# Last stage of a fused attention, MLP and SwiGLU kernel: which queue loads its operands, how many buffers they have, and where the last outputs leave from

## The chip, the cores and the metric

The kernel runs on one core of a Trainium2 chip. Its time is device microseconds from one launch; the time before is 1744.82 us, the median of three runs (1743.07 to 1746.58).

## The reference

Three layers in a row, all in float32:

```python
kv  = einsum('bhsd,bhse->bhde', k, v)              # 8 batches, 8 heads, 576 tokens, 64 wide
out = einsum('bhsd,bhde->bhse', q, kv)
x   = out / sqrt(mean(out**2) + 1e-6) * g_norm     # -> 4608 tokens x 512
h   = x @ w_in                                     # 512 x 2048
x   = (h * clip(h + 3, 0, 6) / 6) @ w_out          # 2048 x 512
g   = x @ w_gate                                   # 512 x 1536
out = (silu(g) * (x @ w_val)) @ w_out2             # 1536 x 512
```

The change lies in the last product, `(...) @ w_out2`, and in what is fetched for it.

## The kernel before, in words

Every float32 operand of a product is split in two, `hi` (rounded to the PE's short float32 form, by ScalarE) and `lo` (the rest, by VectorE), and a product is three matmuls. The layers after the first use a Strassen-like scheme with seven products in place of eight, so the last stage needs seven combinations of the activations: four (`G1`) for its first half, three (`G2`) for its second. The stage before it, `gv_step`, writes these combinations to HBM as `g1d` and `g2d`.

The last stage goes over six blocks of 768 tokens (`j` = 5 down to 0). A block has two halves `h`, a half six steps `q` of two 128-rows each; a step is one *task*, 72 in all. A task of the first half is 24 matmuls of 128x384 (`o2_one`: kinds e, c, d, a), one of the second half 18 (`o2_two`: kinds c, d, a). For each task `g_halves` gets a buffer `graw`, loads it, and splits it: ScalarE makes `gh`, VectorE makes `gl` (lines 107 and 108). `prepare_g(n + 3)` puts this three tasks ahead of the product in the program. Steps 4 and 5 of each half are multiplied together, kind by kind, which needs both loaded.

Before the change `graw` has two buffers and SP's queue issues its loads. The same queue issues the stores of the outputs: `put` transposes an output tile on VectorE (`ot`) and issues four stores; a block has eight tiles, two after its first half (kinds u + v) and six at its end, so 32 stores of 48 KB each.

The matmuls are in the order in which the code issues them. The order on ScalarE, VectorE and the queues is made by a scheduler, and each engine and each queue runs its instructions in that order. The weights of the stage come in six groups of seven tiles (`reload_w2`, 256 KB a tile), named 20 to 25 in the rows; the first two tasks (`g_first`) are loaded one combination at a time into other buffers.

Of the kernel before, what the change touches and what calls it, by code (L numbers as in the profile page):

```python
# [8 lines left out]
F32 = mybir.dt.float32  # L9
F32R = mybir.dt.float32r  # L10
U32 = mybir.dt.uint32
U16 = mybir.dt.uint16
AF = mybir.ActivationFunctionType
ALU = mybir.AluOpType
# [5 lines left out]
def kernel(  # L20
# [27 lines left out]
    nc = tc.nc  # L48
    P = 128
# [5 lines left out]
    KD = DM // P  # L55
# [4 lines left out]
    Q = 32  # L60
# [5 lines left out]
    TH = 384  # L66
    T2 = 2 * TH
    NB2 = NT // T2
    NQ = NF2 // 2
# [17 lines left out]
    wraw = mlp2.enter_context(tc.tile_pool(name="wraw", bufs=3))  # L87
# [14 lines left out]
    def f32(ap):  # L102
        return ap.bitcast(F32)

    def split(hi, lo, src):

        nc.scalar.activation(out=hi, in_=src, func=AF.Copy)  # L107
        nc.vector.tensor_tensor(out=lo, in0=src, in1=f32(hi), op=ALU.subtract)  # L108
# [21 lines left out]
    g1d = dram.tile([NQ, NB2, P, 4, TH], F32, name="g1d")  # L130
    g2d = dram.tile([NQ, NB2, P, 3, TH], F32, name="g2d")
# [22 lines left out]
    def w_slot(name, dtype):  # L154
        return wpool.tile([P, KD, P], dtype, tag="w", name=name)
# [508 lines left out]
    big = {}  # L664
    x_ops = {}

    def load_x1(j):
        x = big["xr"].tile([P, KD, T2], F32, tag="xr", bufs=1, name=f"xr_{j}")
        nc.sync.dma_start(out=x, in_=x1d[:, :, j * T2:(j + 1) * T2])
        return x  # L670
# [49 lines left out]
    G1, G2 = ("T2", "T1", "T3", "B11"), ("T4", "B21", "B22")  # L720
# [67 lines left out]
    def flat(o):  # L788
        return o.rearrange("p k f -> p (k f)")

    def w2_operands(q, tiles):
        w2[q] = {
            key: tuple(flat(o) for o in ops) for key, ops in operands(tiles).items()
        }
# [3 lines left out]
    def slot(name, dtype=F32):  # L798
        return flat(w_slot(name, dtype))

    def g_first(j, q):

        for k, key in enumerate(G1):
            n = f"{key}_{j}_{q}"
            raw, hi, lo = slot(f"ra_{n}"), slot(f"gh_{n}", F32R), slot(f"gl_{n}", F32R)
            nc.sync.dma_start(out=raw[:, :TH], in_=g1d[q, j, :, k])
            split(hi[:, :TH], lo[:, :TH], raw[:, :TH])
            g_ops[j, q, key] = hi[:, :TH], lo[:, :TH]

    def g_halves(j, h, q):  # L810

        n = f"{h}_{j}_{q}"
        keys, src = ((G1, g1d), (G2, g2d))[h]
        m = len(keys)
        raw = big["gr"].tile([P, 4, TH], F32, tag="raw", name=f"graw_{n}")[:, :m]
        nc.sync.dma_start(out=raw, in_=src[q, j])
        hi, lo = (
            big["gy" if h else "gx"].tile([P, m, TH], F32R, tag=f"{h}{o}", name=f"g{o}_{n}")
            for o in "hl"
        )  # L820
        split(hi, lo, raw)
        for k, key in enumerate(keys):
            g_ops[j, q, key] = hi[:, k], lo[:, k]

    acc2 = {}

    def o2_product(j, k, qs, b, a, first):

        ops = [(q, g_ops.pop((j, q, b)), w2[q][a]) for q in qs]
        for i in range(2):  # L830
            cs = slice(i * P, (i + 1) * P)
            for q, g, w in ops:
                for n, (a_, b_) in enumerate(((w[0], g[1]), (w[1], g[0]), (w[0], g[0]))):
                    nc.tensor.matmul(
                        acc2[k][i], a_[:, cs], b_,
                        start=first and q == 0 and n == 0, stop=n == 2, skip_group_check=True,
                    )
            yield i, acc2[k][i]
# [19 lines left out]
                    o, ps_ = ("v", ps) if k == "d" else ("u", acc2["e"][i])  # L858
                    nc.vector.tensor_tensor(out=acc2[o][i], in0=acc2[o][i], in1=ps_, op=ALU.add)

    def put(j, o, dm, i, tok):

        t = slot("ot")[:, :TH]
        nc.vector.transpose(out=t, in_=o)
        r0, c0 = j * T2 + tok * TH, dm * 2 * P + i * P
        for n in range(P // Q):
            nc.sync.dma_start(  # L867
                out=out[r0:r0 + TH, c0 + n * Q:c0 + (n + 1) * Q].rearrange(
                    "(i p) c -> p i c", p=Q
                ),  # L870
                in_=t[n * Q:(n + 1) * Q].rearrange("p (i c) -> p i c", c=Q),
            )

    def o2_two(j, qs):

        for k, b, a, dm, tok in (
            ("c", "B22", "S4", 0, 1), ("d", "T4", "A22", 1, 0), ("a", "B21", "A12", 0, 0),
        ):
            for i, ps in o2_product(j, k, qs, b, a, False):
                if qs[-1] == NQ - 1:  # L880
                    o = slot("o")[:, :TH]
                    if k == "a":
                        nc.scalar.activation(out=o, in_=ps, func=AF.Copy)
                    else:
                        nc.vector.tensor_tensor(out=o, in0=acc2["u"][i], in1=ps, op=ALU.add)
                    put(j, o, dm, i, tok)
        if qs[0] == 0:
            for i in range(2):
                o = slot("o")[:, :TH]
                nc.vector.tensor_tensor(out=o, in0=acc2["u"][i], in1=acc2["v"][i], op=ALU.add)  # L890
                put(j, o, 1, i, 1)
# [4 lines left out]
    with tc.manual_schedule(engines={mybir.EngineType.PE}):  # L896
# [13 lines left out]
        for h in range(2):  # L910
            nc.scalar.dma_start(
                out=gn[h * D:(h + 1) * D, :], in_=g_norm.rearrange("(p o) -> p o", o=1)
            )
        for key, f in (("i", 0), ("i", 1), ("i", 2), ("o", 0), ("i", 3), ("o", 1), ("i", 4)):
            src, ld = (w_in, load_w_cols) if key == "i" else (w_out, load_w_rows)
# [220 lines left out]
        def load_second():  # L1136
            if second:
                kind, p, i = second.pop()
                tiles = load_half(kind, p, i, raw2 if i else None)
                if tiles:  # L1140
                    wgv[kind, p] = operands(tiles)
# [33 lines left out]
        for j in range(1, NB):  # L1175
# [3 lines left out]
            for i, p in enumerate(pairs):  # L1179
# [25 lines left out]
                if j == NB - 1:  # L1205
                    if i == NP1 - 2:
                        parts = prepare_x(0, x1, fpool)
# [36 lines left out]
        JO = list(reversed(range(NB2)))  # L1244
# [8 lines left out]
        def reload_w2(q):  # L1253
            tiles = [w_slot(f"2{q}_{i}", F32R) for i in range(7)]
            for i in (2, 3, 4, 5, 0, 1, 6):
                nc.sync.dma_start(out=flat(f32(tiles[i])), in_=w2d[q, i])
            w2_operands(q, tiles)

        for c, (n, j, p) in enumerate(steps):
            i = c % NH  # L1260
            nxt = visits[n + 1][0] if n + 1 < len(visits) else j
            if i == 0 and nxt != j:
                x1 = load_x1(nxt)
            gv_step(c, j, p, x_ops[j])
            while second:
                load_second()
            if i == NH - 1 and nxt != j:
                *_, x_ops[nxt] = prepare_x(nxt, x1)
            if n < NB2:
                m = (n + 1) % NB2  # L1270
                if i < 2:
                    tiles = load_half(*halves[m], i)
                    if i and m:
                        for k, t in enumerate(tiles):
                            nc.sync.dma_start(
                                out=wsd[m - 1, k], in_=f32(t).rearrange("p k f -> p (k f)")
                            )
                    elif i:
                        wgv[halves[0]] = operands(tiles)
                if n == turn:  # L1280
                    for m in (2 * i + 1, 2 * i + 2):
                        if m < 2 * NH:
                            reload(m)
            else:

                m = c - NB2 * NH
                if m < W2_STEPS:
                    tiles = make_w2(m // 2, m % 2)
                    if tiles:
                        for k, t in enumerate(tiles):  # L1290
                            nc.sync.dma_start(out=w2d[m // 2, k], in_=flat(f32(t)))
            m = c - len(steps)
            if m == -3:
                reload_w2(0)
                g_first(JO[0], 0)
            elif m == -2:
                reload_w2(1)
                g_first(JO[0], 1)
            elif m == -1:
                reload_w2(2)  # L1300
                reload_w2(3)

        mlp2.close()
        big["gr"], big["gy"], big["gx"] = (
            ctx.enter_context(
                tc.tile_pool(name=n, bufs=b, side=o, reuse_waits="tile")
            ) for n, b, o in (("gr", 2, "right"), ("gy", 4, "right"), ("gx", 4, "left"))
        )
        tasks = [(j, h, q) for j in JO for h in range(2) for q in range(NQ)]

        def prepare_g(n):
            if 1 < n < len(tasks):
                g_halves(*tasks[n])

        prepare_g(2)
        reload_w2(4)
        reload_w2(5)
        for n, (j, h, q) in enumerate(tasks):
            prepare_g(n + 3)
            if q < NQ - 2:  # L1320
                (o2_two if h else o2_one)(j, (q,))
            elif q == NQ - 1:
                (o2_two if h else o2_one)(j, (q - 1, q))


# [31 lines left out]
```

## Time and profile before

| what | value |
|---|---|
| time, median of three | 1744.82 us |
| the profiled execution | 1744.33 us, its span 1742.5 us |
| TensorE (PE) busy over the span | 1667.6 us, 96% |
| VectorE (DVE), ScalarE (ACT) busy | 1233.9 us (71%), 890.4 us (51%) |
| mean granted TensorE clock | 0.985 |

The span is what the profiler saw from the first to the last instruction; the rest of the time lies around it. A busy PE is not a PE at full pace: matmuls overlap, and one takes longer at a lower granted clock. In the rows L834 is a matmul of the last stage, L816 a load of `graw`, L867 a store of an output, L1256 a load of a weight tile, SPq is SP's queue.

### The profile page before, as it was taken

The page shows a single profiled execution, that of the slowest core. Times are in us where ns is not written, and L with a number is a line of the kernel's source. Part 1 is how long each engine was busy: PE and PEld are TensorE (multiplying, and loading weights), DVE is VectorE, ACT ScalarE, POOL GpSimd, SP SyncE. Part 2 cuts the span into 40 slices and gives each one's busy share as a digit, 9 for nine tenths or more (in the row PEclk, how much of TensorE's full clock was granted, in tenths as well). Part 3 has the DMA queues.
Part 4 walks back from the last instruction along what each step waited for, and adds up shares of the span by engine and source line. Part 5 has one row for each costly group of instructions (what it writes and reads, how often), then busy time and mean ns, then how long its engine had stood idle before and what let it go on. Part 6 is the DMA issues. An engine that isn't in the chain of part 4 may idle for free.

```text
span 1742.5 us, 27207 instructions
## 1 busy us (share of the span) xinstructions
PE 1667.6 (96%) x9884; PEld 1535.1 (88%) x9884; DVE 1233.9 (71%) x2390; ACT 890.4 (51%) x1647; POOL 2.4 (0%) x7
## 2 busy tenths in 40 slices
PE   8999999999999999999999999999999988888887
PEld 4568899999999999998899999999999987888776
DVE  6888987677777776769897776688876544454444
ACT  5875564545444444446675555466655432332322
POOL 0000000000000000000000000000000000000000
PEclk9999999999999999999999999999999989989999
DMA  8885445454445444254576556866545776656665
GB/s 226 275 261 157 128 144 142 155 140 146 130 148 142 141 134 136 90 176 155 191 257 216 195 197 220 283 226 227 198 173 182 268 237 180 180 172 177 169 179 120
DMA packets 302471, 316.92 MB, mean 182 GB/s; under 512 B 160000, under 2 KB 233216, under 8 KB 302336
## 3 DMA queue, kind: packets, MB, share of 16 engines
q1 hardware_dynamic: 297952, 314.13, 57.8%
q8 instruction: 78, 1.28, 0.3%
q10 hardware_dynamic: 4384, 1.05, 0.3%
q14 instruction: 57, 0.47, 0.1%
HBM read 218.10 MB, written 96.99 MB: 181 GB/s over the span
## 4 chain that ended last, share of the span: by engine, by line
PE 72%; DMA 10%; DVE 9%; ACT 4%; SPq 3%; issue 2%; DVEq 0%; ACTq 0%
PE g L607 15%; PE v L607 15%; PE acc L111 7%; PE acc L112 6%; PE acc L113 6%; PE a L607 6%; DMA graw<-g1d 6%; PE c L607 4%; PE d L607 4%; DMA graw<-g2d 3%; DVE gl L108 3%; SPq L867 2%; ACT gh L107 2%; PE h L117 2%; PE kv L290 1%
## 5 line engine op out<-in xcount | busy, mean ns | idle before, releaser
L108 DVE TENSOR_TENSOR gl<-graw,gh 128x1152 fp32r<-128x1152 f32 (+1 forms) x70 | 108.3, 1549 | 173.6 <-ACT gh L107 173.4
L111 PE MATMUL acc<-g,wo 128*128 128x512 f32 x512 | 202.1, 395 | 0.0
L112 PE MATMUL acc<-g,wo 128*128 128x512 f32 x512 | 199.6, 390 | 0.0
L113 PE MATMUL acc<-g,wo 128*128 128x512 f32 x512 | 199.5, 390 | 0.0
L107 ACT ACTIVATE gh<-graw 128x1152 fp32r<-128x1152 f32 (+1 forms) x70 | 92.3, 1322 | 200.9 <-DMA graw<-g1d 137.4
L652 ACT ACTIVATE t<-h,three 128x512 f32<-128x512 f32 x120 | 86.8, 724 | 141.3 <-DVE h L649 107.6
L107 ACT ACTIVATE g<-t 128x512 fp32r<-128x512 f32 x142 | 89.5, 630 | 65.3 <-DVE t L653 55.0
L108 DVE TENSOR_TENSOR g<-t,g 128x512 fp32r<-128x512 f32 x142 | 96.6, 681 | 31.6 <-ACT g L107 30.8
L113 PEld LDWEIGHTS acc<-g,wo 128*128 128x128 f32 x512 | 96.1, 188 | 20.5
L111 PEld LDWEIGHTS acc<-g,wo 128*128 128x128 f32 x512 | 96.2, 188 | 19.9 <-DVE g L108 0.3
L112 PEld LDWEIGHTS acc<-g,wo 128*128 128x128 f32 x512 | 96.2, 188 | 18.3
L653 DVE SCALAR_TENSOR_TENSOR t<-t,h 128x512 f32<-128x512 f32 x120 | 82.3, 686 | 30.7 <-ACT t L652 29.3
L607 PE MATMUL v<-hT,v 128*128 128x384 f32 x288 | 73.6, 336 | 0.0
L750 DVE TENSOR_TENSOR hg<-hg,g 128x384 f32<-128x384 f32 x36 | 19.9, 552 | 59.4 <-PE g L607 28.1
L108 DVE TENSOR_TENSOR lT<-T,hT 128x384 fp32r<-128x384 f32 x88 | 48.5, 554 | 18.1 <-ACT hT L107 17.7
L760 ACT ACTIVATE hg<-hg 128x768 f32<-128x768 f32 x36 | 30.4, 843 | 58.8 <-DVE hg L752 58.8
L767 ACT ACTIVATE hg<-g 128x384 f32<-128x384 f32 x72 | 35.0, 487 | 49.4 <-PE g L607 49.2
L117 PE MATMUL h<-x,w_i 128*128 128x512 f32 x128 | 57.8, 594 | 1.3 <-DVE w_i L201 0.7
L607 PE MATMUL v<-hB,v 128*128 128x384 f32 x216 | 55.1, 336 | 0.0
L607 PE MATMUL a<-T,wh_i 128*128 128x256 f32 x240 | 53.5, 285 | 1.2 <-ACT s L626 1.1
L607 PE MATMUL c<-T,wh_i 128*128 128x256 f32 x240 | 53.0, 283 | 0.0
L607 PE MATMUL d<-T,wh_i 128*128 128x256 f32 x240 | 53.0, 283 | 0.0
(571 smaller groups left out, 5027.5 us busy)
## 6 DMA issues: line engine op xcount, KB each, us to landing
wo<-wod SPq DMA_DIRECT2D x128, 512.0 KB, 3.5
graw<-g1d SPq DMA_DIRECT2D x34, 768.0 KB, 5.1
g1d<-gt SPq DMA_DIRECT2D x108, 192.0 KB, 2.0
graw<-g2d SPq DMA_DIRECT2D x36, 576.0 KB, 4.1
xr<-x1d SPq DMA_DIRECT2D x10, 1536.0 KB, 6.9
g2d<-hv SPq DMA_DIRECT2D x36, 384.0 KB, 2.4
x1d<-x1o SPq DMA_DIRECT2D x36, 256.0 KB, 2.8
out_dram<-ot SPq DMA_DIRECT2D x192, 48.0 KB, 1.8
```

The lines of the kernel that those rows point to most:

```text
L107: nc.scalar.activation(out=hi, in_=src, func=AF.Copy)
L108: nc.vector.tensor_tensor(out=lo, in0=src, in1=f32(hi), op=ALU.subtract)
L111: nc.tensor.matmul(out_, wh, xl, start=start, stop=False)
L112: nc.tensor.matmul(out_, wl, xh, start=False, stop=False)
L113: nc.tensor.matmul(out_, wh, xh, start=False, stop=stop)
L117: nc.tensor.matmul(out_, f32(w), f32(x), start=start, stop=stop)
L607: nc.tensor.matmul(ps, a[:, kk], b[kk] if isinstance(b, list) else b[:, kk], start=first and n == 0, stop=n == 5, skip_group_check=True,)
L652: nc.scalar.activation(out=t, in_=h[i], func=AF.Relu, bias=three[:, 0:1])
L653: nc.vector.scalar_tensor_tensor(out=t, in0=t, scalar=6.0, in1=h[i], op0=ALU.min, op1=ALU.mult)
L760: nc.scalar.activation(out=hg[:, odd], in_=hg[:, odd], func=AF.Silu)
L767: nc.scalar.activation(out=hg[:, o], in_=ps[0], func=AF.Silu)
L867: nc.sync.dma_start(out=out[r0:r0 + TH, c0 + n * Q:c0 + (n + 1) * Q].rearrange("(i p) c -> p i c", p=Q), in_=t[n * Q:(n + 1) * Q].rearrang ...
```

## The change

The load and the split are parted: `g_load` issues the load on ScalarE's queue one task before the split, into three buffers in place of two. Task 2 of the first block is loaded by `g_early` in two halves, on SP's queue, into buffers that the stage before has in use. The weight groups 20 and 21 are asked for earlier and the first two tasks' loads stand one step differently. Steps 4 and 5 are no longer multiplied together in the first half of the first block, and steps 3 to 5 are in the last half of the last block. In the last block the kind `a` is transposed straight from PSUM, without ScalarE's copy, and five of its eight stores go to ScalarE's queue.

```diff
+    def g_load(j, h, q):
+        m, src = ((4, g1d), (3, g2d))[h]
+        raw = big["gr"].tile([P, 4, TH], F32, tag="raw", name=f"graw_{h}_{j}_{q}")[:, :m]
+        nc.scalar.dma_start(out=raw, in_=src[q, j])
+        graw[j, h, q] = raw
+
+    def g_early(j, h, q):
+        graw[j, h, q] = parts = []
+        for i in range(2):
+            raw = wraw.tile([P, KD, P, 2], U32, tag="raw", name=f"graw_{h}_{j}_{q}_{i}")
+            raw = flat(raw.rearrange("p k c t -> p k (c t)").bitcast(F32))
+            raw = raw[:, :2 * TH].rearrange("p (n t) -> p n t", n=2)
+            nc.sync.dma_start(out=raw, in_=g1d[q, j, :, 2 * i:2 * i + 2])
+            parts.append(raw)
+
     def g_halves(j, h, q):
         n = f"{h}_{j}_{q}"
-        keys, src = ((G1, g1d), (G2, g2d))[h]
+        keys, raw = (G1, G2)[h], graw.pop((j, h, q))
         m = len(keys)
-        raw = big["gr"].tile([P, 4, TH], F32, tag="raw", name=f"graw_{n}")[:, :m]
-        nc.sync.dma_start(out=raw, in_=src[q, j])
...
-        split(hi, lo, raw)
+        if isinstance(raw, list):
+            for i, r in enumerate(raw):
+                split(hi[:, 2 * i:2 * i + 2], lo[:, 2 * i:2 * i + 2], r)
+        else:
+            split(hi, lo, raw)
...
+    JO_END = 0
...
-    def put(j, o, dm, i, tok):
+    def put(j, o, dm, i, tok, queues=(0, 0, 0, 0)):
...
-        for n in range(P // Q):
-            nc.sync.dma_start(
+        for n, e in enumerate(queues):
+            (nc.sync, nc.scalar)[e].dma_start(
...
-                    o = slot("o")[:, :TH]
-                    if k == "a":
-                        nc.scalar.activation(out=o, in_=ps, func=AF.Copy)
+                    end = k == "a" and j == JO_END
+                    if end:
+                        o = ps
                     else:
-                        nc.vector.tensor_tensor(out=o, in0=acc2["u"][i], in1=ps, op=ALU.add)
-                    put(j, o, dm, i, tok)
+                        o = slot("o")[:, :TH]
+                        if k == "a":
+                            nc.scalar.activation(out=o, in_=ps, func=AF.Copy)
+                        else:
+                            nc.vector.tensor_tensor(out=o, in0=acc2["u"][i], in1=ps, op=ALU.add)
+                    put(j, o, dm, i, tok, (1, 0, 1, 1 - i) if end else (0, 0, 0, 0))
...
             m = c - len(steps)
-            if m == -3:
+            if m == -6:
                 reload_w2(0)
+            elif m == -4:
+                reload_w2(1)
+            elif m == -3:
                 g_first(JO[0], 0)
             elif m == -2:
-                reload_w2(1)
                 g_first(JO[0], 1)
+                g_early(JO[0], 0, 2)
+                reload_w2(2)
             elif m == -1:
-                reload_w2(2)
                 reload_w2(3)
...
-            ) for n, b, o in (("gr", 2, "right"), ("gy", 4, "right"), ("gx", 4, "left"))
+            ) for n, b, o in (("gr", 3, "right"), ("gy", 4, "left"), ("gx", 4, "right"))
...
         def prepare_g(n):
+            if 2 < n + 1 < len(tasks):
+                g_load(*tasks[n + 1])
             if 1 < n < len(tasks):
                 g_halves(*tasks[n])
...
+            group.append(q)
+            together = 1 if n < NQ else 3 if n >= len(tasks) - NQ else 2
+            if q < NQ - together or q == NQ - 1:
+                (o2_two if h else o2_one)(j, tuple(group))
+                group = []
```

What this does to the order is seen on SP's queue first, where block 5 ends and block 4 begins (`graw_4_1` is block 4, step 1; `ot` are output tiles). Before:

```order
L816 DMA graw_4_0_16311<-g1d 128x1536
L816 DMA graw_4_1_16335<-g1d 128x1536
L816 DMA graw_4_2_16341<-g1d 128x1536
L867 DMA out_dram<-ot 32x12x32 x24
L816 DMA graw_4_3_16431<-g1d 128x1536
L816 DMA graw_4_4_16469<-g1d 128x1536
```

The load of step 3 stood behind the 24 stores of the block's end. Now SP's queue, from the last weight tiles to its end:

```order
L1282 DMA 25_5_16020<-w2d 128x512
L1282 DMA 25_0_16015<-w2d 128x512
L1282 DMA 25_1_16016<-w2d 128x512
L1282 DMA 25_6_16021<-w2d 128x512
L889 DMA out_dram<-ot 32x12x32 x187
```

Nothing but stores is left on it, 187 of 192. The loads are on ScalarE, here where block 4 ends and block 3 begins (L107 is the split's `gh`, L909 the copy of kind a; DMAHW is one of eight semaphores that the transfers of both queues take in turn):

```order
L816 DMA graw_3_1_16725<-g1d 128x1536 [waits DMAHW7_49,DVE_49]
L816 DMA graw_3_2_16749<-g1d 128x1536 [waits DMAHW2_49,DVE_49]
L107 ACTIVATE gh_3_1_16751<-graw_3_1_16725 128x1536 [waits DMAHW7_49]
L816 DMA graw_3_3_16755<-g1d 128x1536 [waits DMAHW4_49,DVE_49]
L107 ACTIVATE gh_3_2_16757<-graw_3_2_16749 128x1536 [waits DMAHW2_49]
L816 DMA graw_3_4_16845<-g1d 128x1536 [waits DMAHW0_49,DVE_49]
L107 ACTIVATE gh_3_3_16847<-graw_3_3_16755 128x1536 [waits DMAHW4_49]
L909 ACTIVATE o<-o2a_4_16443 128x384 [waits PE_49]
L816 DMA graw_3_5_16883<-g1d 128x1536 [waits DMAHW5_49,DVE_49]
L909 ACTIVATE o<-o2a_4_16444 128x384 [waits PE_49]
```

A load now stands between the splits of the two tasks before it, and the two copies of kind a stand behind the split of step 3; before, they stood ahead of it.

At the entry to the stage SP's queue had, behind the last store of the stage before (`gt_35`):

```order
L756 DMA g2d<-gt_35_15940 128x384
L1256 DMA 24_0_15995<-w2d 128x512
L1256 DMA 24_1_15996<-w2d 128x512
L1256 DMA 24_6_16001<-w2d 128x512
L816 DMA graw_5_2_15989<-g1d 128x1536
L1256 DMA 25_2_16011<-w2d 128x512
```

and has now:

```order
L756 DMA g2d<-gt_35_15958 128x384
L1282 DMA 23_6_15968<-w2d 128x512
L1282 DMA 24_2_16003<-w2d 128x512
L1282 DMA 24_3_16004<-w2d 128x512
L1282 DMA 24_4_16005<-w2d 128x512
L1282 DMA 24_5_16006<-w2d 128x512
```

Fifteen weight tiles now follow that store, where ten did; task 2 is no longer among them.

## Rows read from the trace of the kernel before

**Rows 1.** Busy time of each engine by stretch; columns as in its first line.

```profile
core 0: us, PE busy (x) PEld busy (x) DVE busy (x) ACT busy (x) POOL busy (x), PEclk, DMA share, GB/s
...
1350.00:1394.00 44.00, 44.00 (x253) 44.00 (x252) 24.13 (x44) 19.13 (x40) 0.00 (x0) 1.00 0.78 268
...
1394.00:1732.00 338.00, 287.08 (x1517) 279.20 (x1515) 161.75 (x180) 107.31 (x106) 0.00 (x0) 0.93 0.63 180
...
1440.00:1460.00 20.00, 19.98 (x114) 19.56 (x113) 11.47 (x14) 6.39 (x6) 0.00 (x0) 1.00 0.73 191
1460.00:1480.00 20.00, 12.18 (x59) 11.54 (x58) 6.54 (x4) 5.50 (x4) 0.00 (x0) 0.83 0.55 168
```

**Rows 2.** PE's waits from 1390 us on: us in total, times, longest.

```profile
PE o2e L834 <- DVE gl L108: 42.5, 13, 6.5
PE o2c L834 <- DVE gl L108: 6.5, 5, 1.8
```

**Rows 3.** SP's queue in order of time, first block's end: start, us, instruction.

```profile
1447.11 0.32 SPq L816 DMA_DIRECT2D graw<-g1d  x1
1448.19 12.67 SPq L867 DMA_DIRECT2D out_dram<-ot  x24
1460.96 8.88 SPq L816 DMA_DIRECT2D graw<-g1d  x3
```

**Rows 4.** ScalarE in order of time, the same place.

```profile
1466.21 1.48 ACT L107 ACTIVATE gh<-graw 128x1536 fp32r<-128x1536 f32 x1 [12.28 <-DMA graw<-g1d]
```

**Rows 5.** PE in order of time, the stage's first tasks.

```profile
1394.62 0.33 PE L834 MATMUL o2e<-gl_T,20_2_15614 128*128 128x384 f32 x1
...
1402.77 0.34 PE L834 MATMUL o2a<-gh_B,21_0_15778 128*128 128x384 f32 x1
1407.76 0.69 PE L834 MATMUL o2e<-gl,22_2_15946 128*128 128x384 f32 x1 [4.65 <-DVE gl L108]
...
1411.77 0.52 PE L834 MATMUL o2d<-gl,22_4_15948 128*128 128x384 f32 x1
```

**Rows 6.** Groups by line and form: busy us, mean ns, idle before and releaser.

```profile
L108 DVE TENSOR_TENSOR gl<-graw,gh 128x1536 fp32r<-128x1536 f32 x34 | 59.6, 1753 | 109.2 <-ACT gh L107 109.0
L107 ACT ACTIVATE gh<-graw 128x1536 fp32r<-128x1536 f32 x34 | 50.5, 1487 | 137.4 <-DMA graw<-g1d 137.4
L107 ACT ACTIVATE gh<-graw 128x1152 fp32r<-128x1152 f32 x36 | 42.0, 1166 | 63.5 <-DMA graw<-g2d 63.4
```

**Rows 7.** DMA from 1400 to 1743 us: queue share; issues, KB, median us to landing.

```profile
q1 hardware_dynamic: 87997, 59.45, 62.2%
...
graw<-g1d SPq DMA_DIRECT2D x33, 768.0 KB, 5.1
graw<-g2d SPq DMA_DIRECT2D x36, 576.0 KB, 4.1
out_dram<-ot SPq DMA_DIRECT2D x192, 48.0 KB, 1.8
```

**Rows 8.** The chain that ended last: loads under way while stores were issued.

```profile
1494.04 6.66 DMA graw<-g1d
...
1551.97 6.83 DMA graw<-g1d
```

**Rows 9.** Issues on ScalarE's own queue, early in the kernel: ns min/median/max.

```profile
L258 ACTq DMA_DIRECT2D q<-in_q_dram x8: 374/416/542, 0.7 to 10.2; - x8
```

**Rows 10.** SP's queue, then ScalarE, at the entry to the stage.

```profile
1398.05 0.32 SPq L816 DMA_DIRECT2D graw<-g1d  x1
...
1401.97 0.40 SPq L1256 DMA_DIRECT2D 25_6_16015<-w2d  x1
...
1404.43 1.48 ACT L107 ACTIVATE gh<-graw 128x1536 fp32r<-128x1536 f32 x1 [10.16 <-DMA graw<-g1d]
```

**Rows 11.** The chain's and SP's last rows.

```profile
1729.86 2.13 PE o2a L834 x12
...
1731.05 9.32 SPq L867 DMA_DIRECT2D out_dram<-ot  x18
```

More of the change, by code (lines that the diff above doesn't have):

```diff
@@ L808, in g_first @@
             g_ops[j, q, key] = hi[:, :TH], lo[:, :TH]
+    graw = {}
+    def g_load(j, h, q):
[11 more added lines that the diff above has]
+            parts.append(raw)
     def g_halves(j, h, q):
         n = f"{h}_{j}_{q}"
-        keys, src = ((G1, g1d), (G2, g2d))[h]
+        keys, raw = (G1, G2)[h], graw.pop((j, h, q))
         m = len(keys)
-        raw = big["gr"].tile([P, 4, TH], F32, tag="raw", name=f"graw_{n}")[:, :m]
-        nc.sync.dma_start(out=raw, in_=src[q, j])
         hi, lo = (
@@ L1317 @@
         reload_w2(5)
+        group = []
         for n, (j, h, q) in enumerate(tasks):
             prepare_g(n + 3)
[L1320 to L1323, printed above, removed]
+            group.append(q)
+            together = 1 if n < NQ else 3 if n >= len(tasks) - NQ else 2
+            if q < NQ - together or q == NQ - 1:
+                (o2_two if h else o2_one)(j, tuple(group))
+                group = []
 _INS = [
```

## The prediction

> **What bounds the kernel now.** I read the busy times by stretch first, then PE's waits, then the two queues in order of time where PE waits, and the DMA view last.
>
> Up to 1394 us PE bounds the kernel: in the last 44 us before it PE is busy for all of them at the full granted clock, 253 matmuls, 0.1739 us each [rows 1]. Nothing that the change does to other engines there can gain anything; it could only lose.
>
> From the first matmul of the last stage at 1394.62 us [rows 5] to PE's end at 1729.86 + 2.13 = 1731.99 us [rows 11] it is another matter. The stage has 6 x (6 x 24 + 6 x 18) = 1512 matmuls. In its best 20 us one takes 19.98 / 114 = 0.1753 us [rows 1], so the work is between 1512 x 0.1739 = 262.9 and 1512 x 0.1753 = 265.1 us; I take 264.0. The stage takes 337.4, so 73.4 us are lost. Two rows name 42.5 + 6.5 = 49.0 us of waits, all for `gl`, the VectorE half of the split [rows 2]. The other 24.4 us are pace: in the stage the mean granted clock is 0.93 [rows 1], and after a wait of 4.65 us the next 12 matmuls take 1411.77 - 1407.76 = 4.01 us, 0.334 each, nearly twice 0.1739, which is the pace of the lower level, 1.2 GHz [rows 5]. So each waited us costs half a us more: 24.4 / 49.0 = 0.50.
>
> Why is `gl` late? VectorE waited for `gh`, and `gh` waited 137.4 + 63.4 us for loads [rows 6]. And the loads? On SP's queue a load is issued at 1447.11, then come the 24 stores of a block's end, 12.67 us of them, because they wait for tiles and take 0.52 us each (9.32 / 18 [rows 11]); the next load goes out at 1460.96 [rows 3]. ScalarE stood 12.28 us for it [rows 4], and in that 20 us stretch PE was busy for 12.18 us [rows 1]. So it is a queue in order, not the data rate: in the stage the 16 DMA engines were busy 62.2% of 343 us, 213 us [rows 7], and 213 is under 264.
>
> **The change part by part.**
>
> *Loads on ScalarE's queue, three buffers.* The stores no longer stand ahead of a load. What bounds a load now? On ScalarE's order a load is issued after the split of two tasks back, so two are under way at a time, and a pair of tasks takes issue + landing + `gh`. With the medians, 0.42 us for an issue on this queue [rows 9], landings of 5.1 and 4.1 us [rows 7] and splits of 1.49 and 1.17 us [rows 6], a task needs (0.42 + 5.1 + 1.49) / 2 = 3.5 us in the first half and (0.42 + 4.1 + 1.17) / 2 = 2.85 in the second. PE needs 24 x 0.1746 = 4.19 and 18 x 0.1746 = 3.14. PE is the longer in both, so in the steady part loads run ahead until they wait for buffers. ScalarE has room: 107.31 us busy in 338 [rows 1], plus 69 issues x 0.42 = 29.
>
> The landing of a load beside stores of the other queue is the disputed cost. The nearest rows are loads under way while SP issued stores: 6.66 and 6.83 us [rows 8]. I take the medians for the steady part and 6.8 us at a block's end, since 24 of 32 stores leave there; with 6.8 everywhere rival B follows.
>
> The Trainium skill (DMA: Bandwidth & Descriptors, section "Issuing engines are not separate DMA queues") says that transfers started by different engines run on the same 16 DMA engines and interleave, and that a second issuer only saves the sequencer's time to issue. The rows agree with its first half as far as they go, 62.2% busy with one queue; for the second, what stood in line here was the issue itself, and by the rule at its strictest, no load landing sooner and stores slowing them, the time is rival B's.
>
> *Entry to the stage.* Before, task 2's load was issued at 1398.05 and its split began at 1404.43 [rows 10]; PE stood 4.65 us [rows 5], and a second time for tasks 4 and 5 together. Now task 2 is loaded in the stage before, and task 3's load goes out at the same place, about 1398.1, when the buffers of the stage before are free. The weight tiles behind it are 15, not 10, so I keep the landing of before, 6.4 us, and add 0.8 (5 x 256 KB at the 268 GB/s of [rows 1] would be 4.9 us if all of them stood ahead of it; most are issued after it). `gh` then ends at 1406.8, `gl` (1.75 [rows 6]) at 1408.6. PE, three tasks at 4.17 us, is through at 1394.6 + 12.5 = 1407.1: it waits 1.5 us, between 0 and 5. Tasks 4 and 5 are now multiplied apart, so the second wait goes.
>
> *A block's end, four times.* In ScalarE's order the two copies of kind a stand behind the split of step 3, and PE's next block needs those banks. Call the block's end B. Step 1's split comes some 4 us ahead of it, step 3's load behind that, at B - 3.9. With 6.8 us it lands at B + 2.9, is split by B + 4.4, the first copy (0.49) is done at B + 4.9, the second behind another issue at B + 5.8. PE comes to kind a of the next block after 18 matmuls, at B + 3.1, and waits about 1.8 + 0.4 = 2.2 us; with the median landing of 5.1 it waits 0.1. I take 1.5 a time, 6.0 in all, bounds 0.4 and 8.8. What is queued behind those copies on ScalarE are the next splits; they are some 8 us early and lose nothing.
>
> *The last block.* SP's last 18 stores ran from 1731.05 to 1740.37, 8.4 us past PE's end, and the span ends at 1742.5, 10.5 past it [rows 11]. Now 19 of its last 24 stores are SP's. Steps 3 to 5 together make a kind 18 matmuls, 3.14 us, so the first tile of kind c is there 7.8 us before PE's end and leaves about 6.6 before it; 19 x 0.52 = 9.9 us later, 3.3 us past PE's end, SP has issued all, and with the same 2.1 us behind that the span ends 5.4 past. ScalarE's five issues end earlier. Transposing from PSUM has no row; even at twice the ordinary time it would delay two tiles that SP reaches last anyway.
>
> *At nothing:* the earlier weight loads and the two early loads of task 2. Their cover is the stage before, where the DMA engines are busy 0.78 at the end and PE is never short [rows 1]: 0.8 MB more comes in there, and the 3.7 MB of weight groups 20 and 21 are asked for earlier. Without that cover PE would stand some 2 to 5 us.
>
> **Sum.** 1394.6 + 264.0 + (1.5 + 6.0) x 1.50 for waits with their share of slower pace = 1669.9 for PE's end; + 5.4 = 1675.3 for the span. Around the span lie 1744.33 - 1742.5 = 1.8 us, and the median of the runs is 0.5 over the profiled one: 1677.6, say **1677 us**, 3.9% faster.
>
> **Rivals.**
>
> *B: loads and stores slow each other and loads set the pace.* If every load takes 6.8 us as under the stores of [rows 8] (5.5 for the smaller), a task needs 4.36 and 3.55 us, a block 6 x 7.91 = 47.4 against PE's 44.0, 3.4 x 6 = 20 us more idle time, 30 with the slower pace, less what the block's ends would have waited anyway (9): about 1698. For it: the same bytes must now pass in a fifth less time, so the 62.2% becomes about 77% (213 / 275). Against: the stretch ahead of the stage runs at 0.78 and 268 GB/s with PE full [rows 1], and buffers hold several us of lead over a burst of stores.
>
> *C: loads still tied to the stores.* Transfers of both queues take eight semaphores in turn, and a load waits for the one that had its semaphore before, often a store. If the program waits there as it did in the queue, little is won but the end: about 1744.8 - 5 = 1740, the change not doing what it says. Against: the semaphore that a load at a block's end waits for belongs to that block's first stores or to older ones.
>
> *D: ScalarE becomes the bound and the kernel is slower.* All loads, splits and copies now stand in one order, and a load that waits holds the splits behind it. Before, a block took 337.4 / 6 = 56.2 us. A block by loads takes 6 x (L1 + L2 + 3.5) / 2, which passes 56.2 when both landings together pass 15.2 us, 1.65 times the 9.2 of [rows 7]; with the 5 us won at the end, from about 15.5. At twice the landings, 18.4, a block is 65.7 us, the stage 57 us longer: about 1797. For it: landings have gone to 6.8; against: none near 8.
>
> **How the numbers follow.** The sum's case 0.62, B 0.30, C 0.03, D 0.03, the rest 0.02 about where it was. The time predicted is the sum's. Its own range: no waits and 262.9 us of work give 1665, the upper bounds of entry and block ends 1687. B goes to some 1702 if the waits fall badly. The range is 1663 to 1702, which leaves out 2 in 10 at most. A measurement here tells 0.2%, 3.5 us, from no change: faster by more than that 0.95, within it 0.02, slower 0.03.
>
> **What would show it.** Right: PE's waits in the stage under 20 us in all and the granted clock over 0.97 there; SP's queue with stores only, ScalarE's loads never more than a few us behind a store; PE's waits at each block's end on ScalarE's copy L909 and not on `gl`; the span's end some 5 us past PE's. Wrong: waits on `gl` in every block (B), with landings near 7 us or over; ScalarE idle before its loads until a store lands (C); landings over 8 us (D); a PE wait before 1394 us, which would show that the early loads have no cover.

## The result, and the profile after

The changed kernel takes 1673.38 us (median of 4 runs, 1671.85 to 1674.75), the kernel before on the same chip 1743.94 (4 runs, 1741.58 to 1746.58). The ratio is 0.9595, 95% interval 0.9578 to 0.9612: 4.05% faster, where 1677 us, 3.9%, was forecast. The profiled execution took 1674.75 us, its span is 1673.0.

PE's waits from 1200 us to the end (total, times, longest):

```profile
PE o2e L856 <- DVE gl L108: 3.2, 1, 3.2
```

The kernel before had 50.9 us of them. [rows 2] shows the two groups for `gl`, 49.0 us; its list has two more, which the prediction left out:

```profile
PE o2d L834 <- DVE o L885: 1.4, 3, 0.7
PE o2a L834 <- ACT o L883: 0.5, 1, 0.5
```

Where the one wait that is left is, in PE's timeline (start, length, then the idle time before it and what ended it):

```profile
1410.50 0.52 PE L856 MATMUL o2e<-gl,23_2_15964 128*128 128x384 f32 x1 [3.15 <-DVE gl L108]
```

It is task 3 of block 5, at the entry to the stage. From there to its last matmul PE stands still no more. Busy times by stretch, in the columns of [rows 1]:

```profile
1350.00:1394.00 44.00, 44.00 (x253) 44.00 (x252) 24.61 (x46) 20.72 (x43) 0.00 (x0) 1.00 0.62 210
1400.00:1420.00 20.00, 16.84 (x87) 16.52 (x87) 7.77 (x6) 5.92 (x5) 0.00 (x0) 0.91 0.95 348
1420.00:1440.00 20.00, 20.00 (x117) 20.00 (x116) 14.05 (x18) 10.53 (x12) 0.00 (x0) 1.00 0.86 280
1440.00:1460.00 20.00, 20.00 (x115) 20.00 (x114) 14.83 (x15) 9.26 (x9) 0.00 (x0) 1.00 0.91 245
1660.00:1673.00 13.00, 4.67 (x27) 4.35 (x26) 3.43 (x6) 0.00 (x0) 0.00 (x0) 0.76 0.57 84
```

The first row has PE busy for 44.00 of 44 us. The two early loads of task 2 themselves go out sooner, at 1242.65 and 1266.24 us, and the list of waits has none there either: they cost PE nothing. The second is the entry, with the DMA engines at 0.95. Then PE is full at the full granted clock, 2.4 GHz, also at 1440 to 1460, the stretch in which a block ends. The last row is the end, where PE is done and stores leave.

The DMA view from 1400 to 1673 us (queue: packets, MB, share of the 16 engines; then issues: count, KB each, median us to landing), to be held against [rows 7]:

```profile
q10 hardware_dynamic: 11936, 47.44, 52.6%
q1 hardware_dynamic: 76646, 12.55, 25.8%
graw<-g1d ACTq DMA_DIRECT2D x32, 768.0 KB, 5.9
graw<-g2d ACTq DMA_DIRECT2D x36, 576.0 KB, 4.8
out_dram<-ot SPq DMA_DIRECT2D x187, 48.0 KB, 3.4
```

The engines are busy 78% instead of 62, and everything lands later than before: loads 5.9 and 4.8 us instead of 5.1 and 4.1, stores 3.4 instead of 1.8. PE doesn't see it. What became of the wait for loads is told by ScalarE's waits over the stage:

```profile
ACT gh L107 <- DMA graw<-g1d: 45.8, 22, 6.9
ACT gh L107 <- DMA graw<-g2d: 36.4, 22, 3.9
ACT gh L107 <- PE o2a L856: 29.6, 13, 3.7
```

ScalarE still waits 82 us for loads (201 in [rows 6]), but the third row is new: 29.6 us it waits for PE to free a buffer of split operands. An engine that waits for its consumer is ahead of it.

### The profile page after: what moved, and what is told of

The parts are those of the page before. It is cut to its first block, busy times and chain, and to the rows that moved or that the text cites. A ratio compares the mean times of both kernels' runs of the same rounds, so it can differ in the third digit from the quotient of the medians.

```text
span 1673.0 us, 27253 instructions
## 1 busy us (share of the span) xinstructions
PE 1647.2 (98%) x9884; PEld 1522.7 (91%) x9884; DVE 1235.8 (74%) x2391; ACT 891.2 (53%) x1646; POOL 2.4 (0%) x7
## 4 chain that ended last, share of the span: by engine, by line
PE 90%; DVE 4%; DMA 3%; ACT 1%; issue 1%; SPq 0%; DVEq 0%; ACTq 0%
PE g L607 16%; PE v L607 16%; PE acc L111 7%; PE acc L112 7%; PE acc L113 7%; PE a L607 7%; PE c L607 4%; PE o2c L856 4%; PE d L607 4%; PE o2a L856 4%; PE o2d L856 4%; PE h L117 2%; PE o2e L856 2%; PE kv L290 1%; DMA raw_v<-in_moe_w_val_dram 1%
## 5 line engine op out<-in xcount | busy, mean ns | idle before, releaser
L108 DVE TENSOR_TENSOR gl<-graw,gh 128x1152 fp32r<-128x1152 f32 (+2 forms) x71 | 107.7, 1524 | 75.6 <-ACT gh L107 75.4
L107 ACT ACTIVATE gh<-graw 128x1152 fp32r<-128x1152 f32 (+2 forms) x71 | 92.0, 1306 | 121.3 <-DMA graw<-g1d 45.8
L107 ACT ACTIVATE g<-t 128x512 fp32r<-128x512 f32 x142 | 89.5, 630 | 65.4 <-DVE t L653 55.0
L760 ACT ACTIVATE hg<-hg 128x768 f32<-128x768 f32 x36 | 30.3, 843 | 58.2 <-DVE hg L752 58.2
```

The source lines that it names most:

```text
L760: nc.scalar.activation(out=hg[:, odd], in_=hg[:, odd], func=AF.Silu)
```

## The experiments

All times are medians. The kernel before ran beside each group of runs, at 1743.99 to 1744.45. "Stage" is the time from the first matmul of the last stage to the end of the last one in the profiled execution, read from PE's timeline: 337.4 us before (with 50.9 us of waits), 270.1 after (3.2). (Its start lies between 1392.5 and 1394.6 in these executions and differs by 0.8 us between two of the changed kernel itself, so the stage is the better yardstick.)

| version | time, us | ratio, interval | PE waits, us | stage, us |
|---|---|---|---|---|
| changed kernel, again | 1672.66 | 0.9590, 0.9577–0.9603 | 2.3 | 269.2 |
| before + ScalarE's queue | 1694.34 | 0.9715, 0.9696–0.9735 | 15.0 | 286.4 |
| before + three buffers | 1710.68 | 0.9810, 0.9794–0.9826 | 26.9 | 306.4 |
| before + both | 1678.43 | 0.9626, 0.9610–0.9642 | 5.3 | 272.2 |
| changed, two buffers | 1691.48 | 0.9701, 0.9685–0.9717 | 19.0 | 290.7 |
| changed, loads on SP | 1687.20 | 0.9681, 0.9666–0.9696 | 13.4 | 282.5 |
| changed, no early pair | 1676.31 | 0.9615, 0.9598–0.9631 | 6.4 | 274.1 |
| changed, old end | 1675.05 | 0.9604, 0.9591–0.9618 | 2.7 | 268.9 |
| changed, even end | 1671.42 | 0.9581, 0.9568–0.9594 | 3.8 | 269.9 |
| changed, both ends | 1669.55 | 0.9573, 0.9560–0.9586 | 2.3 | 269.5 |
| changed, half the stores | 1672.56 | 0.9591, 0.9577–0.9606 | 2.7 | 269.0 |

The theory of the prediction was that the lost time is a queue in order: a load late because stores stand ahead of it. The rival that I set against it is lookahead: two buffers let too few loads run at a time, whatever the queue.

**Before, loads on ScalarE's queue, nothing else.**

```diff
-        nc.sync.dma_start(out=raw, in_=src[q, j])
+        nc.scalar.dma_start(out=raw, in_=src[q, j])
```

> The kernel before with one word changed: the loads of the last stage are issued by ScalarE, two buffers, each load written right ahead of its split; entry, grouping and end as before. In ScalarE's order two loads stand ahead of two splits. Theory 'queue': waits only at the entry (about 12 us with pace) and the old end: about 1687. Theory 'lookahead': a pair of tasks takes issue, landing, two gh and what is left of gl, 8.75 us in the first half and 6.9 in the second against PE's 8.4 and 6.3; 18 x (0.4+0.6) = 18 us, 27 with pace, plus entry 12 and the old end: about 1713. Rival D of the prediction (ScalarE's order bound, slower than before): over 1750, landings over 8 us. I expect about 1710.

One word wins 50 us of the 71. It came out between the two theories, nearer to the queue's; the 1710 that I expected was 16 us too slow. The rest is in PE's waits:

```profile
PE o2e L834 <- DVE gl L108: 10.1, 5, 2.4
PE o2a L834 <- ACT o L883: 3.9, 3, 2.6
PE o2c L834 <- DVE gl L108: 1.0, 1, 1.0
```

Task 3, which waited 5.6 to 6.5 us in each block from the second on before, doesn't wait any more. Left are 4.7 us at the entry, waits of 1.0 to 1.9 us on tasks 4 and 5, and the second row, which comes back below. The period of a pair of tasks doesn't explain that. With the landings measured here, 4.7 and 4.0 us, it would be 8.35 against PE's 8.4 in the first half, where most of these waits are, and 6.8 against 6.3 in the second, where there is only one, of 1.0 us.

**Before, three buffers; and both together.**

```diff
-            ) for n, b, o in (("gr", 2, "right"), ("gy", 4, "right"), ("gx", 4, "left"))
+            ) for n, b, o in (("gr", 3, "right"), ("gy", 4, "left"), ("gx", 4, "right"))
```

> The kernel before with three buffers for raw operands instead of two; loads stay on SP's queue, each written right ahead of its split, entry, grouping and end as before. In SP's order the 24 stores of a block's end still stand ahead of the load of task 3 of the next block. Theory 'queue' (a load behind 24 stores is late whatever the buffers): 12 us of waits a block stay, about 1740. Theory 'lookahead' (each of the two halves, buffers and queue, wins most by itself): 1690 to 1700, as with loads on ScalarE's queue and two buffers. A load that stands behind the stores cannot use a third buffer, so I expect 1730 to 1742.

This edit also swaps the sides of the two other pools, as the whole change does; that was not tried apart. (The version above, with the old sides, and the changed kernel with two buffers, with the new ones, differ by 2.9 us, no more than the early pair and the new end are worth below.)

The expectation missed: 1711, 33 us faster, by neither theory's number. SP's timeline and PE's, where block 5 ends, show why:

```profile
1433.79 2.97 SPq L816 DMA_DIRECT2D graw<-g1d  x2
1440.53 12.28 SPq L867 DMA_DIRECT2D out_dram<-ot  x24
1452.91 1.38 SPq L816 DMA_DIRECT2D graw<-g1d  x3
```

```profile
1461.62 0.44 PE L834 MATMUL o2e<-gl,23_2_15960 128*128 128x384 f32 x1 [4.40 <-DVE gl L108]
```

The 24 stores keep the next load back for 12.28 us, as before [rows 3]. But the three loads behind them now go out within 1.38 us, where [rows 3] has 8.88 for three, and by the traces task 3's goes out 8.6 to 9.4 us after PE's start on the block, not 10.2 to 11.7. So there are six waits in the stage, 26.9 us: one at the entry and one of 3.6 to 5.0 us on task 3 of each later block. Those on tasks 4 and 5, which came to 11.4 us before (without the entry), are gone. My expectation took a late load for a late PE and left out the lead, and the loads behind the late one.

> The kernel before with the loads issued by ScalarE and three buffers, and nothing else of the change: no early pair, old grouping, old end. It fills the fourth corner beside the kernel before (1744), three buffers alone (1711) and ScalarE's queue alone (1694). If the two halves of the remedy serve the same wait, the corner lies near the changed kernel plus the price of its other edits as measured (no early pair +3.6, old end +2.4) plus 1 to 4 us for the pair of tasks at the entry: 1679 to 1683, and 65 of the 71 us come from queue and buffers together, where 33 + 50 = 83 would be their plain sum. In ScalarE's order the second copy of a block's end stands behind the split of task 3 here (in the changed kernel ahead of it), so waits on the copies at block ends may appear, up to 2 us each; without any the time is at the lower end.

1678.43, just under the range: both together make 65.8 us of the 70.6, with no wait but 5.3 us at the entry. One alone is worth 33, the other 50, and their plain sum would be too much, because they overlap. Of the 50.9 us of waits before, 30.3 were on task 3 after a block's end: the queue alone takes them all away, three buffers alone 8.1 of them. The 11.4 on tasks 4 and 5 go with three buffers alone, and nearly half of them with the queue alone.

**The changed kernel with one half taken back.**

```diff
-            ) for n, b, o in (("gr", 3, "right"), ("gy", 4, "left"), ("gx", 4, "right"))
+            ) for n, b, o in (("gr", 2, "right"), ("gy", 4, "left"), ("gx", 4, "right"))
```

> The changed kernel with two buffers for raw operands instead of three; loads stay on ScalarE's queue. Theory 'queue' (the 73 us were loads standing behind stores, and any load on a queue of its own keeps them): no change to the changed kernel's 1673, at most 5 us more. Theory 'lookahead' (two buffers cannot feed PE, whichever queue): a buffer is held for issue 0.35, landing, gh 1.49 and gl 1.75 us, so with landings of 5.1 and 4.1 a task needs (0.35+5.1+3.24)/2 = 4.35 and (0.35+4.1+2.3)/2 = 3.4 us against PE's 4.19 and 3.14; 6 x 6 x (0.16+0.26) = 15 us of waits, 23 with the slower pace, about 1696; with landings of 5.9 and 4.8, as now, 4.75 and 3.75, 42 to 63 us, 1715 to 1736. Waits on gl spread over all blocks. I expect 1696.

18 us slower than the changed kernel: "queue alone" (at most 5) falls. "Lookahead" is right that two buffers are too few, and its sum of 23 comes near, but by luck. It stands on landings of 5.1 and 4.1 us; with 4.7 and 3.9 as measured here the same working gives 36 x 0.135 = 4.9 us of waits, 7 with the slower pace, all in the second halves. PE's waits on `gl` are 14.5 us instead, six on task 5 of the first halves and two in the second halves of the first and the last block, and there is a new row:

```profile
PE o2e L856 <- DVE gl L108: 10.4, 6, 2.7
PE o2a L856 <- ACT o L909: 4.5, 5, 1.6
PE o2c L856 <- DVE gl L108: 4.1, 2, 3.2
```

The second is the wait at a block's end that the prediction had priced: five times, 0.9 us on the mean. ScalarE around the end of block 5 (at 1442.07), and PE's wait:

```profile
1443.04 0.47 ACT L909 ACTIVATE o<-o2a 128x384 f32<-128x384 f32 x1
1445.59 1.49 ACT L107 ACTIVATE gh<-graw 128x1536 fp32r<-128x1536 f32 x1 [2.08 <-DMA graw<-g1d]
1445.95 0.33 ACTq L816 DMA_DIRECT2D graw<-g1d  x1
1446.98 0.47 ACT L909 ACTIVATE o<-o2a 128x384 f32<-128x384 f32 x1
```

```profile
1447.51 0.44 PE L856 MATMUL o2a<-gl,20_0_15176 128*128 128x384 f32 x1 [1.57 <-ACT o L909]
```

The second copy stands behind a split that waits for its load, and ends at 1447.45; PE goes on at 1447.51. The changed kernel, where block 4 ends (at 1487.76):

```profile
1480.45 0.33 ACTq L816 DMA_DIRECT2D graw<-g1d  x1
1483.74 1.49 ACT L107 ACTIVATE gh<-graw 128x1536 fp32r<-128x1536 f32 x1 [1.87 <-DMA graw<-g1d]
1485.97 1.49 ACT L107 ACTIVATE gh<-graw 128x1536 fp32r<-128x1536 f32 x1 [0.73 <-DMA graw<-g1d]
1487.37 0.47 ACT L909 ACTIVATE o<-o2a 128x384 f32<-128x384 f32 x1
1489.74 0.49 ACT L909 ACTIVATE o<-o2a 128x384 f32<-128x384 f32 x1 [1.91 <-DVE gl L108]
```

Here the load of step 3 went out 7.3 us ahead of the block's end, its split was done before the end, and the second copy ends at 1490.23, 0.7 us before PE asks for that bank at 1490.94.

```diff
-        nc.scalar.dma_start(out=raw, in_=src[q, j])
+        nc.sync.dma_start(out=raw, in_=src[q, j])
```

> The changed kernel with the loads put back on SP's queue; three buffers, the early pair, the grouping and the end stay. In SP's order a block's 24 stores now stand behind the load of task 3 of the next block and ahead of the load of task 4 (before: ahead of task 3's). Theory 'queue alone': most of the gain is lost, 1725 or more, with a wait in every block. Theory 'both': the load of task 4 is issued some 9 us past the block's end, lands some 6 later, gl is ready at about 18.4 us past the end where PE asks at 16.8; 5 waits of about 1.7, with pace about 13 us: about 1686. Theory 'lookahead alone': 1673 to 1676 and no waits. In all, waits on gl fall in the first half of blocks.

14 us slower, with waits on tasks 4 and 5, at the size that "both" gave (13). In part that is luck. One thing I had not reckoned: 6.1 of the 13.4 us are a wait at the entry, where a load now stands behind the weight tiles of group 25 on SP's queue. The other eight waits are 0.5 to 1.1 us each, 7.3 in all, where "both" had 8.5.

**The two ends of the stage.**

```diff
-                g_early(JO[0], 0, 2)
...
+            if n == 2:
+                g_load(*tasks[2])
             if 2 < n + 1 < len(tasks):
                 g_load(*tasks[n + 1])
```

> The changed kernel without the early pair: task 2 is loaded at the stage's entry on ScalarE's queue like the others. PE asks for task 2 at 1394.6 + 8.35 = 1403.0. If the early pair is worth something: the load goes out at about 1399.05, lands 8 us later, gl is ready at about 1410.5, PE waits some 7.5 us instead of 3.15, and the time is 4 to 7 us more, about 1679. If it is worth nothing: 1673, with a wait on task 2 no longer than the 3.15 us that task 3 costs now.

1676.31, and 6.4 us of waits instead of 3.15: the early pair is worth 3 to 3.6 us, a little under the lower bound of 4.

```diff
-                    end = k == "a" and j == JO_END
+                    end = False
...
-            together = 1 if n < NQ else 3 if n >= len(tasks) - NQ else 2
+            together = 1 if n < NQ else 2
```

> The changed kernel without its edits to the last block: tasks in pairs up to the end, kind a copied by ScalarE, all stores on SP's queue. If the prediction's account of the end holds (it is SP's issue of the last 24 stores that counts), the first of them leaves about 4 us before PE's end instead of 6.6, and 24 at 0.52 to 0.66 us each end 8.5 to 12 us past PE's end, with 2.1 behind them: the span ends 10.5 to 14 past PE's end where it is 8.3 now, 1675.5 to 1678.5. If the end is set by the last landing and not by the issues: no more than 1 us over the base.

1675.05 against 1672.66, just under the range. The span ends 10.6 us past PE's end instead of 8.2 in the base, with 24 stores of 0.51 us:

```profile
1658.95 12.29 SPq L889 DMA_DIRECT2D out_dram<-ot  x24
```

```diff
-                    put(j, o, dm, i, tok, (1, 0, 1, 1 - i) if end else (0, 0, 0, 0))
+                    put(j, o, dm, i, tok, {
+                        "c": (0, 0, 0, 0), "d": (1, 1, 1, 1), "a": (1, 0, 1, 1) if i else (0, 0, 0, 0),
+                    }[k] if j == JO_END else (0, 0, 0, 0))
```

> The changed kernel with the last 24 stores shared evenly: SP takes kind c, half 0 of kind a and one of half 1 (13), ScalarE kind d and three of half 1 (11). SP is held up by 19 issues of 0.66 us now. If issue is what sets the end: SP's 13 end at about 1667.0 of the profiled execution and ScalarE's 11 at 0.4 to 0.5 us by 1666.8, with 2.1 us behind them the span ends at 1669, 4 us sooner: 1669.5. If the 16 DMA engines set it (48 KB in runs of 128 bytes, whichever queue), less than 1 us.

The span ends 6.2 us past PE's end, 2 us better and not 4; the time is 1.2 us less, and its interval overlaps the base's. The reason is in ScalarE's timeline, shown from the next version, which has the same end:

```profile
1659.50 7.04 ACTq L893 DMA_DIRECT2D out_dram<-ot  x11
```

Its 11 stores take 0.64 us each, not 0.4 to 0.5, and land 2.7 us after issue, not 1.8. So issue is part of the end, and here each of the two queues issued more slowly than SP alone did (0.51); why, these runs don't show.

```diff
-        for i in range(2):
+        for i in range(2 if q == 2 else 1):
             raw = wraw.tile([P, KD, P, 2], U32, tag="raw", name=f"graw_{h}_{j}_{q}_{i}")
...
                 g_early(JO[0], 0, 2)
+                g_early(JO[0], 0, 3)
```

(`g_load` then fetches only the other two parts of task 3, on top of the even end.)

> The even tail and, at the entry, half of task 3 (2 of its 4 parts, 384 KB) loaded early as well, in the third buffer that the stage before leaves free; the other half goes out where task 3's load goes now. The entry's wait of 3.15 us is for task 3's load, which takes 8.1 us beside the weights. If it is the bytes that make it late: half of it lands 1.5 to 3 us sooner, the wait falls to 0 to 1.5 us but task 4, which lands right behind it, may ask for up to 1.5 us instead; 1.5 to 3 us less than the even tail alone, about 1667. If the entry is bound by the data rate up to task 4 (the weights of group 24 and 25 in front of it), the wait only moves to task 4 and nothing is won.

1669.55 (1668.58 to 1670.88), against 1672.66 (1672.08 to 1672.99) for the changed kernel beside it: the lowest of all, though its range overlaps that of the even end alone. What is shown of it is the end. At the entry the wait on `gl` is gone, but the stage is no shorter (269.5 us; 269.2 in the base). A wait stands further on instead, so this is the second case of the expectation, with a copy in the place of task 4:

```profile
1421.29 0.44 PE L860 MATMUL o2c<-gl,20_4_15180 128*128 128x384 f32 x1 [2.31 <-ACT v L882]
```

PE now waits for a copy of kind c, which stands behind three splits on ScalarE that waited for loads. The same wait, of 0.9 to 1.1 us, is in three versions with the changed kernel's entry (old end, even end, half the stores), beside one on `gl`. From 1400 to 1410 us the DMA engines are at 1.04 by the profile and 402 GB/s, and at 1.03 and 400 in the base: there is no room left in that stretch, with half of task 3 loaded early or not.

**Half the stores.**

```diff
         for n, e in enumerate(queues):
+            if n % 2 and j != JO_END:
+                continue
```

> The changed kernel with half of the output stores of blocks 5 to 1 left out (two of four for each tile, so these parts of the output are not written); the last block stores all. If loads and stores share the engines' time, the loads' median landings fall from 5.9 and 4.8 towards 5.1 and 4.1, and the stores' 3.4 towards 1.8. The time stays where it is, within 2 us of 1673, if PE is the bound and the loads have lead enough; it falls by more than 5 us if the stores still cost PE something that its waits do not show.

The time doesn't move. The landings of loads go from 5.7 and 4.7 us in the base to 5.6 and 4.4, and the stores' from 3.6 to 3.5. So it is hardly the stores' bytes that lengthen a load; with two buffers instead of three they are 4.7 and 3.9, with all the stores there. What differs there is how many loads run at a time. By issue and landing in the traces one load is under way for 72% of the time with two buffers, and two for 22%; in the changed kernel two are for half of the time, and three hardly ever. In the base a 768 KB load issued with no other under way lands after 4.4 us (median of 6), with one under way after 5.8 (of 24).

## Why the prediction was right, point by point

- **What bounds the kernel, and that it is a queue.** Right, but half the account. The stores' place in the queue was the larger single cause (50 us when it alone is removed); the third buffer's 33 us was in the diff and in the title of the part, but my text gave the whole cause to the queue. The full account: a load is late only if it is late beyond the lead that the buffers hold. A reading was short, too: the waits before were 50.9 us and not all for `gl`, so 22.5 us of the 73.4 lost were pace, 0.44 for each waited us.
- **Pairs of loads, 3.5 and 2.85 us a task.** The conclusion (no waits in the steady part) is right, the working is not. I left `gl` out of a buffer's time, though it reads the raw operands too. With it and the measured landings a task of the first half needs (0.35 + 4.7 + 1.49 + 1.75) / 2 = 4.15 us with two buffers, which leaves nothing to PE's 4.19, and (0.35 + 5.9 + 1.49 + 1.75) / 3 = 3.2 with three. Such periods still don't say where the waits of the version with two buffers fall.
- **Work 264.0 us.** 270.06 less 3.15 of wait, and half as much again of slow pace (1.6), leaves 265.3: 1.3 low, just past the upper bound of 265.1.
- **Entry 1.5 us.** It was 3.15 in the profiled execution, 2.3 in the second; within 0 to 5. (The first two tasks' loads stand in the same steps as before, by the diff; it is weight group 22 that moved by one.) The load took 8.09 us, the longest DMA piece in the stage's chain of work:

```profile
1396.06 2.92 DMA g2d<-gt
1399.05 8.09 DMA graw<-g1d
1410.50 2.12 PE o2e L856 x6
```

- **Block ends 6.0 us.** This term failed: measured 0, below its lower bound of 0.4. The mechanism is real, as the version with two buffers shows, but I timed it with step 3's load going out 3.9 us ahead of the block's end; with three buffers it goes out 6.5 to 8.8 us ahead. The sign that I had named for being right, PE's waits at a block's end on the copy L909, is absent. The lead that I counted on in the steady part I did not carry to the block's end.
- **Price of a wait, 1.5 us each.** Near for long waits: from the stages and waits of before and after, (337.4 - 270.1) / (50.9 - 3.2) = 1.41; three buffers alone, with waits of 3.6 to 5.0 us, gives (306.4 - 270.1) / (26.9 - 3.2) = 1.53, ScalarE's queue alone (286.4 - 270.1) / (15.0 - 3.2) = 1.38. It is lower where the added waits are short or few: 1.30 with two buffers, 1.22 with the loads on SP, 1.25 without the early pair.
- **End 5.4 us past PE's.** It was 8.3. SP's 19 stores took 12.55 us, not 9.9. SP's timeline in the middle of them:

```profile
1663.56 0.48 SPq L889 DMA_DIRECT2D out_dram<-ot  x1
1666.15 1.89 SPq L889 DMA_DIRECT2D out_dram<-ot  x4
```

  Between 1664.04 and 1666.15 SP waits 2.1 us, by the list of waits for another store to land. ScalarE's first store goes out at 1663.76 and stores on its queue take 1.8 us, so this fits a store of SP's that takes over a semaphore from one of ScalarE's: rival C's mechanism, in one place. Which semaphore it was the trace doesn't show, and it wasn't tried with other semaphores.
- **The sum.** PE's end 1664.7, forecast 1669.9: -9.0 for block ends with their pace, +2.5 for the entry, +1.3 for work, together -5.2. The span's end gives +2.9 back. The two errors of size partly cancel, so 1675.3 against 1673.0 flatters the working.
- **Rivals.** B did not come: landings rose to 5.9, not 6.8, and no block waits. Its reason was wrong too, since stores hardly lengthen loads. The 6.66 and 6.83 us of [rows 8], on which its price stood, were misread: those loads were not issued among stores but 0.5 us behind another load, when the burst was out. SP's queue before, for the first of them:

```profile
1489.32 4.11 SPq L867 DMA_DIRECT2D out_dram<-ot  x8
1493.53 0.42 SPq L816 DMA_DIRECT2D graw<-g2d  x1
1494.04 0.38 SPq L816 DMA_DIRECT2D graw<-g1d  x1
```

  C: SP's stores now wait for loads through the shared semaphores, 42.9 + 16.8 us by its list of waits, but it is the stores that wait; ScalarE's list puts one wait, of 2.7 us, down to a store, and PE's none. D: the landings together are 10.7 us, far from 15.5.
- **The rule.** The Trainium skill (DMA: Bandwidth & Descriptors, section "Issuing engines are not separate DMA queues") says that a second issuer saves only the time to issue, usually small. The trace agrees with the other half of that section, that both run on the same engines: their shares are 52.6 and 25.8%, and landings are later. On this half the measurement decides: here one word that moved the issue was worth 50 us, because what stood in line was an issue behind 24 others, 12.67 us [rows 3], and not its own 0.4.

## What to carry to other kernels

Where transfers of two kinds share an issuing queue in order, look in its timeline at what stands ahead of each load, and then count how many buffers of lead the consumer has at that moment: a load behind a 12 us burst cost PE 5.6 to 6.5 us a block with two buffers, and more on the tasks behind it, but 3.6 to 5.0 with three and nothing more. Queue and depth are remedies that overlap, so test each alone and both together before you credit either. Once PE has no waits inside a stage, what is left lies at its ends; where one was removed there, at the entry, another stood further on and the stage was no shorter.

## What the runs showed of the hardware that I had not expected

- A store of 48 KB in runs of 128 bytes lands after 1.8 us when loads and stores share SP's queue (1.9 in the changed kernel with its loads put back on SP), and after 3.1 to 3.9 us when the loads are on ScalarE's, with the same bytes and even with half the stores (3.5). Much of this is not the queue but whether a load is under way. By issue and landing in the traces, a store issued while no load is under way takes 1.8 to 1.9 us in every version. With one under way it takes 2.6 to 3.0 us on the shared queue, where 42 to 65 of the 192 stores meet a load, and 3.6 to 4.6 with the loads on ScalarE's, where 120 to 135 do. Why it is longer there too stays open.
- SP issues such stores at 0.51 us each alone (12.29 / 24). With ScalarE issuing too, 13 took 8.77 us on SP and 11 took 7.04 on ScalarE, 0.67 and 0.64 each. The even end is not free of the shared semaphores, so how much of this is the issue itself stays open.
